# Splitting the last accumulated first-weight part directly on ScalarE and VectorE

## The chip, the cores and the metric

The kernel runs on one core of a Trainium2 chip. The metric is the device time of one launch in microseconds (us), the median over runs; the runs of the kernel before lie between 389.09 and 389.71 us. Smaller is better. A profiled execution gives the trace that is read below.

## The reference, cut to what matters

```python
x = A_x                                   # (1, 2048, 512)
xn = _layernorm(x, axis=-1)
s = irfft2(rfft2(xn) * (w_r + 1j*w_i))    # over tokens and channels
h = _layernorm(xn, axis=-1)
u = gelu(einsum("bsd,sf->bdf", h, w1) + b1)   # (1, 512, 1792)
y = einsum("bdf,fs->bds", u, w2) + b2
return x + s * silu(y.transpose(0, 2, 1))
```

Two branches share the normalised input: a spectral filter `s` (transform, multiply, transform back) and a two-layer perceptron over the token axis, whose first product is `h` by `w1` and whose second is by `w2`. All of it is in float32; the large products are made of three products of a high and a low part each.

## The kernel before, in words

The 2048 tokens are 16 tiles `j` of 128 partitions. Of the 14 column blocks of `w1` (128 columns each), seven are accumulated in the first stage, while the tiles of `x` are loaded, normalised and transformed. The other seven follow in the second stage, in two batches: `w1` is cut into 32 parts `i`, part `i` being tile `i % 16` of batch `i // 16`. A part of the second batch has 384 columns in two runs: block 6 (128 columns) and blocks 12 and 13 (256 columns). It is used by three tiles of products on TensorE (`hidden`), each of three matmuls: high by high, high by low of `h`, and low by high, in this order. The last four parts are kept and used at the end of the stage, one block after the other (lines L146 to L148).

A part needs a high half `wh` (`w1h` in the trace) and a low half `wl` (`w1l`), made from the raw weights `w` (`w1s`, three buffers) that SyncE's queue loads. There are two ways to make them, in `w1_part`:

```python
            if i in ADDED:
                A.activation(wh, w, AF.Copy)
                A.activation(wl, wh.bitcast(F32), AF.Copy, scale=-1.0)
                w1_runs(i, wl, G, accum_op=ALU.add)
                return wh, wl
            split(wh, wl, w)
```

With `split`, ScalarE rounds the high half (L143) and VectorE subtracts it from the raw weights (L143). With `ADDED`, ScalarE also writes the negated high half into `wl` (L484), and two DMAs from GpSimd's queue add the raw weights to it from memory once more (L344 on POOL). Parts 10, 12, ... 22 take the second way in the kernel before.

The parts are asked for by `hidden_rest`, three ahead of use. The order of the second stage is written out by hand: the tables `PACE` and `LAST` say how many tiles of products go between the steps of the spectral filter. The filter works on eight pairs of frequency groups, `filter_pair(n)`, with items 2n and 2n+1. Of an item, ScalarE copies `px` out of PSUM (L567); SyncE's queue exchanges partitions of it with four DMAs `xc<-px` (L573); GpSimd's queue loads the factors `wt` (L564); VectorE works through L587 to L598, with the multiplication by `wt` at L591 and the last step at L598; TensorE multiplies back with `hf,xc` (64 matmuls for a pair, the first 32 of its first item). Between these steps VectorE and ScalarE make the forms of the activated hidden layer (`forms`: `fa`, `fb`, `fc`, `fd` at L301 and L302, `u` at L321 to L324).

At the end of the second stage SyncE's queue, behind the last `w1s` loads, loads four tiles of `w2` (L696); GpSimd's queue adds a second piece of `w2` to two of them (L698). From these ScalarE and VectorE make `w2f` (L707, L708) for the third stage, which is the product with `w2`, the gate and the output.

Each engine runs its instructions in program order, and so does each DMA queue when it issues.

Of the kernel before, what the change touches and what calls it, by code (L numbers as in the profile page):

```python
# [26 lines left out]
PACE = [(2, 2, 2, 1, 1, 1)] * 4 + [(2, 2, 2, 2, 1, 1)] * 4  # L27
LAST = (4, 4, 4, 4, 4)
MADE = (3, 3, 3, 3, 3, 3, 2, 2)
ADDED = range(10, 24, 2)  # L30
WARM = 16
TAIL = 4
LATE = 12
# [101 lines left out]
def spectral_mixer_kernel(tc, x, w1, b1, w2, b2, wk, we, wx, c_f, c_ft, c_d, c_i, c_g, c_h, out):  # L135
# [14 lines left out]
    with tc.tile_pool(name="ps", bufs=1, space=PSUM) as psp, ExitStack() as left, ExitStack() as right:  # L150
# [322 lines left out]
        def w1_part(i):  # L473
# [7 lines left out]
            wh, wl = (w1p.tile([P, 4 * P], F32R, name=f"w1{c}{runs[0][0]}_{j}", tag="w1" + c)[:, :n] for c in "hl")  # L481
            if i in ADDED:
                A.activation(wh, w, AF.Copy)
# [407 lines left out]
```

## Time and profile before

| | |
|---|---|
| time, median of 3 runs | 389.25 us (389.09 to 389.71) |
| span of the profiled execution, first to last instruction | 387.8 us |
| median less span | 1.4 us |
| PE busy | 375.9 us (97%) |
| DVE busy | 323.3 us (83%) |
| ACT busy | 228.2 us (59%) |
| POOL busy | 78.4 us (20%) |
| DMA | 70.03 MB, mean 181 GB/s |

The profiled execution is known by its span alone; what lies around it is taken as the 1.4 us by which the median of the runs exceeds the span. The first stage lasts to about 97 us of the span, the second to about 215 us, the third to the end. PE, PEld, DVE, ACT, POOL and SP in the views are TensorE's matmuls, its weight loads, VectorE, ScalarE, GpSimd and SyncE; a `q` behind the name is the queue from which an engine issues DMAs. In rows of the timeline the first number is the start in the span, the second the duration, and a bracket at the end is the idle time ahead of the instruction with what ended it.

### The profile page before, as it was taken

How to read it: one execution, taken by the hardware profiler on the slowest of the kernel's cores; microseconds unless marked ns; L12 is line 12 of the kernel's file. 1: busy time of each engine (PE TensorE's matmuls, PEld its weight loads, DVE VectorE, ACT ScalarE, POOL GpSimd, SP SyncE). 2: the span in 40 equal slices, each digit the busy share in tenths (PEclk: the TensorE clock that was granted, in tenths of full speed). 3: DMA queues.
4: the chain of work that ended last, by engine and by line, in shares of the span. 5: the costliest groups of instructions: out<-in, count | busy, mean ns of one | idle time of the engine just before them, and what ended most of it. 6: DMA issues, size and time to landing. Idle time of an engine off the chain costs nothing.

```text
span 387.8 us, 8067 instructions
## 1 busy us (share of the span) xinstructions
PE 375.9 (97%) x2936; PEld 330.1 (85%) x2936; DVE 323.3 (83%) x734; ACT 228.2 (59%) x412; POOL 78.4 (20%) x133
## 2 busy tenths in 40 slices
PE   7999999999999999999699989999999999999995
PEld 4888888888777887777488979999999999999994
DVE  6899999976679998996985999797878798787873
ACT  4676776674843465575326795565656564746541
POOL 3133323221203233332001003020202020110100
PEclk9999999999999999999789999999999999999999
DMA  8965777312626889988928388997968779795602
GB/s 262 309 238 168 258 241 248 91 55 86 206 64 179 209 237 266 231 214 211 234 67 246 54 241 214 209 225 161 227 147 217 134 206 177 208 160 162 103 2 55
DMA packets 39144, 70.03 MB, mean 181 GB/s; under 512 B 5424, under 2 KB 21440, under 8 KB 38976
## 3 DMA queue, kind: packets, MB, share of 16 engines
q1 hardware_dynamic: 30048, 48.14, 39.9%
q0 software_dynamic: 9056, 21.38, 28.9%
q8 instruction: 23, 0.38, 0.4%
q14 instruction: 17, 0.14, 0.1%
HBM read 61.10 MB, written 8.13 MB: 179 GB/s over the span
## 4 chain that ended last, share of the span: by engine, by line
PE 82%; DVE 7%; DMA 4%; issue 4%; ACT 1%; POOL 1%; DVEq 0%; POOLq 0%; ACTq 0%
PE ps L829 27%; PE ps L132 24%; PE ps L377 20%; PE ps L241 4%; PE ps L764 3%; DVE w2f L708 2%; DMA out_dram<-g 2%; DMA w1l<-in_w_dram 2%; PE ps L147 2%; PE ps L366 1%; PE ps L148 1%; PE ps L146 1%; ACT w2f L707 1%; POOL w1l L344 1%; DVE cl L143 0%
## 5 line engine op out<-in xcount | busy, mean ns | idle before, releaser
L377 PE MATMUL ps<-h,w1h 128*128 128x512 f32 x224 | 58.7, 398 | 0.0
L132 PE MATMUL ps<-h,w1h 128*128 128x512 f32 x152 | 50.1, 412 | 0.0
L708 DVE TENSOR_TENSOR w2f<-s,w2f 128x896 fp32r<-128x896 f32 x32 | 34.8, 1091 | 16.3 <-ACT w2f L707 15.7
L377 PEld LDWEIGHTS ps<-h,w1h 128*128 128x128 f32 x224 | 40.9, 188 | 7.9
L829 PE MATMUL ps<-fa,w2f 128*128 128x256 f32 x336 | 43.4, 282 | 0.0
L829 PE MATMUL ps<-fb,w2f 128*128 128x256 f32 x336 | 42.5, 281 | 0.1
L829 PE MATMUL ps<-fc,w2f 128*128 128x256 f32 x336 | 41.5, 281 | 0.9 <-DVE w2f L708 0.6
L829 PEld LDWEIGHTS ps<-fa,w2f 128*128 128x128 f32 x336 | 41.6, 188 | 0.8
L829 PEld LDWEIGHTS ps<-fc,w2f 128*128 128x128 f32 x336 | 40.3, 188 | 1.4 <-DVE w2f L708 0.8
L829 PEld LDWEIGHTS ps<-fb,w2f 128*128 128x128 f32 x336 | 40.4, 188 | 0.5 <-DVE c L799 0.5
L698 POOL DMA_DIRECT2D s<-in_w_dram x16 | 13.9, 869 | 125.1 <-DVE es L769 42.6
L707 ACT ACTIVATE w2f<-s 128x896 fp32r<-128x896 f32 x32 | 30.1, 949 | 13.9 <-DVE s L721 11.0
L132 PEld LDWEIGHTS ps<-h,w1h 128*128 128x128 f32 x152 | 28.0, 194 | 10.2 <-issue 5.0
L708 DVE TENSOR_TENSOR w2f<-a,w2f 128x896 fp32r<-128x896 f32 x24 | 26.1, 1086 | 10.1 <-ACT w2f L707 10.1
L132 PE MATMUL ps<-h,w1l 128*128 128x512 f32 x76 | 30.7, 403 | 3.3 <-DMA w1l<-in_w_dram 3.3
L377 PE MATMUL ps<-h,w1l 128*128 128x512 f32 x112 | 30.6, 390 | 0.0
L707 ACT ACTIVATE w2f<-a 128x896 fp32r<-128x896 f32 x24 | 22.8, 951 | 12.1 <-PE ps L829 7.4
L377 PEld LDWEIGHTS ps<-h,w1l 128*128 128x128 f32 x112 | 21.0, 188 | 4.5
L590 DVE SCALAR_TENSOR_TENSOR xc<-xc,turn,px 128x512 f32<-128x512 f32 x32 | 23.9, 747 | 0.0
L372 DVE TENSOR_TENSOR w1l<-w1r,w1h 128x512 fp32r<-128x512 f32 (+1 forms) x32 | 20.7, 648 | 2.4 <-ACT w1h L369 2.2
L805 POOL DMA_DIRECT2D out_dram<-g x15 | 13.4, 896 | 42.3 <-DVE g L803 42.3
L795 ACT ACTIVATE g<-c,b2t 128x256 f32<-128x256 f32 x24 | 12.1, 505 | 15.6 <-DVE c L799 13.1
(128 smaller groups left out, 765.8 us busy)
## 6 DMA issues: line engine op xcount, KB each, us to landing
a<-in_w_dram SPq DMA_DIRECT2D x24, 448.0 KB, 3.9
wt<-in_wk_dram POOLq DMA_DIRECT2D x16, 512.0 KB, 5.1
s<-in_w_dram SPq DMA_DIRECT2D x16, 448.0 KB, 4.3
s<-in_w_dram POOLq DMA_DIRECT2D x16, 448.0 KB, 6.3
w1s<-in_w_dram SPq DMA_DIRECT2D x36, 128.0 KB, 3.3
w1r<-in_w_dram SPq DMA_DIRECT2D x16, 256.0 KB, 3.7
xc<-px SPq DMA_DIRECT2D x64, 64.0 KB, 4.1
x<-in_x_dram SPq DMA_DIRECT2D x15, 256.0 KB, 4.0
```

The source lines that it names most:

```text
L132: return lambda *args, **kw: self.keep(operation(*args, **kw))
L241: T.matmul(z[:, b], h[:, b * P:(b + 1) * P], c, start=True, stop=True)
L372: keep(V.tensor_sub(dst, src, hi.bitcast(F32)))
L377: T.matmul(ps[:, bank + i], w[wi][:, i * P:(i + 1) * P], hj, start=first and j == 0, stop=last and j == NJ - 1)
L590: V.scalar_tensor_tensor(to, zt, turn[:, k:k + 1], px[:, ::-1], op0=ALU.mult, op1=ALU.add)
L698: G.dma_start(t, w2_half(*added), accum_op=ALU.add)
L707: A.activation(wf[:, 0], v, AF.Copy)
L708: V.tensor_sub(wf[:, 1], v, wf[:, 0].bitcast(F32))
L764: T.matmul(pe[:, b % 2, b // 2], yt[:, b], ci[:, b], start=True, stop=True)
L795: A.activation(g[:, cols], src, AF.Silu, bias=b2t[:, j:j + 1], scale=scale)
L805: G.dma_start(out[:, j, cols], g[:, cols], accum_op=ALU.add)
L829: T.matmul(o, wf[:, wi, i], ui, start=m + a == 0 and n in (1, 2, 5), stop=m == NH - 1 and a == 2, skip_group_check=n in (6, 3, 7, 4))
```

## The change

One number of a table changes, so that part 22 (tile 6 of the second batch) is no longer in `ADDED`:

```diff
-ADDED = range(10, 24, 2)
+ADDED = range(10, 22, 2)
```

For part 22 one ScalarE activation (L484) and two accumulating DMAs of GpSimd's queue (L344; 64 and 128 KB) go, and one VectorE subtraction of 128x384 (L143) comes. The scheduler places it, and moves one other instruction. In the names below the last number is that of a buffer, and the number before it the tile or the item: `w1l6_6` is the low half of part 22, `w1s6_9` the raw weights of part 25.

On VectorE the new subtraction stands among the steps of items 12 and 13 of the spectral filter (a piece of the difference):

```order
 L590 SCALAR_TENSOR_TENSOR xc12_2267<-xc12_2267,turn_67,px12_2265 128x512
 L591 TENSOR_TENSOR xc12_2267<-xc12_2267,wt12_2211 128x1024
+L143 TENSOR_TENSOR w1l6_6_2380<-w1s6_6_2376,w1h6_6_2379 128x384
 L592 TENSOR_TENSOR xc12_2267<-xc12_2267 128x512
 L587 TENSOR_TENSOR s1_13_2329<-xc13_2276,e1_76 128x2
```

It was put behind the multiplication of item 12, ahead of everything that is left of items 12 and 13.

Further on in VectorE's order, where item 13 ends and the forms of `u3` begin, before:

```order
L598 TENSOR_TENSOR xc13_2276<-s1_13_2329 128x2
L323 SCALAR_TENSOR_TENSOR u3_1535<-u3_1535 128x256
L324 SCALAR_TENSOR_TENSOR u3_1535<-u3_1535 128x256
L302 TENSOR_TENSOR fc3_2756<-u3_1535,fc3_2756 128x2x256
L143 TENSOR_TENSOR w1l6_8_2490<-w1s6_8_2486,w1h6_8_2489 128x384
L302 TENSOR_TENSOR fb3_2755<-u3_1535,fb3_2755 128x2x256
L587 TENSOR_TENSOR s1_14_2473<-xc14_2432,e1_76 128x2
```

And the same place in the changed kernel:

```order
L598 TENSOR_TENSOR xc13_2276<-s1_13_2329 128x2
L323 SCALAR_TENSOR_TENSOR u3_1535<-u3_1535 128x256
L324 SCALAR_TENSOR_TENSOR u3_1535<-u3_1535 128x256
L143 TENSOR_TENSOR w1l6_8_2488<-w1s6_8_2484,w1h6_8_2487 128x384
L302 TENSOR_TENSOR fc3_2754<-u3_1535,fc3_2754 128x2x256
L302 TENSOR_TENSOR fb3_2753<-u3_1535,fb3_2753 128x2x256
L587 TENSOR_TENSOR s1_14_2471<-xc14_2430,e1_76 128x2
```

The subtraction of part 24 (`w1l6_8`) moved ahead of `fc3`; ScalarE's high half of part 24 moved ahead of its own `fc3` in the same way.

On SyncE's queue nothing is moved, but a wait changes. Its order before, from the loads of part 24 on, with the semaphores that each row waits for in brackets:

```order
L344 DMA w1s6_8_2486<-in_w1_dram 128x128 [waits DMAHW0_49,DVE_49]
L344 DMA w1s6_8_2486<-in_w1_dram 128x256 [waits DMAHW1_49]
L344 DMA w1s6_9_2514<-in_w1_dram 128x128 [waits DMAHW2_49,Activation_49]
L344 DMA w1s6_9_2514<-in_w1_dram 128x256 [waits DMAHW3_49]
L585 DMA hf14_2471<-in_c_h_dram 128x128 [waits DMAHW4_49,PE_49]
L751 DMA cd_64<-in_c_i_dram 128x512 [waits DMAHW5_49]
L585 DMA hf15_2496<-in_c_h_dram 128x128 [waits DMAHW6_49,PE_49]
L573 DMA xc14_2432<-px14_2430 32x512 [waits DMAHW7_49,Activation_49]
```

And in the changed kernel:

```order
L344 DMA w1s6_8_2484<-in_w1_dram 128x128 [waits DMAHW0_49,DVE_49]
L344 DMA w1s6_8_2484<-in_w1_dram 128x256 [waits DMAHW1_49]
L344 DMA w1s6_9_2512<-in_w1_dram 128x128 [waits DMAHW2_49,DVE_49]
L344 DMA w1s6_9_2512<-in_w1_dram 128x256 [waits DMAHW3_49]
L585 DMA hf14_2469<-in_c_h_dram 128x128 [waits DMAHW4_49,PE_49]
L751 DMA cd_64<-in_c_i_dram 128x512 [waits DMAHW5_49]
L585 DMA hf15_2494<-in_c_h_dram 128x128 [waits DMAHW6_49,PE_49]
L573 DMA xc14_2430<-px14_2428 32x512 [waits DMAHW7_49,Activation_49]
```

The load of part 25 takes the raw buffer of part 22. It waited for ScalarE, which read that buffer last; now it waits for VectorE's subtraction. Behind it on the queue stand the loads `hf14`, `cd` and `hf15` and the exchanges `xc14` and `xc15`.

## The prediction

> **What bounds the kernel now.** I read the engine table of the page first, then the waits and TensorE's timeline in the second half of the second stage, then the timeline of the queue that TensorE waited for, and the windows for the granted clock.
>
> ```profile
> PE 375.9 (97%) x2936; PEld 330.1 (85%) x2936; DVE 323.3 (83%) x734; ACT 228.2 (59%) x412; POOL 78.4 (20%) x133
> ```
>
> TensorE is nearly always busy, so one looks for its few waits. The longest behind the start is at the part that the change touches.
>
> ```profile
> 184.48 0.61 PE L132 MATMUL ps<-h,w1h 128*128 128x512 f32 x2
> ...
> 185.16 0.61 PE L132 MATMUL ps<-h,w1h 128*128 128x512 f32 x2
> 188.44 0.47 PE L132 MATMUL ps<-h,w1l 128*128 128x512 f32 x1 [2.67 <-DMA w1l<-in_w_dram]
> ...
> 190.00 0.80 PE L132 MATMUL ps<-h,w1l 128*128 128x512 f32 x1 [0.62 <-DMA w1l<-in_w_dram]
> 190.72 1.99 PE L132 MATMUL ps<-hf,xc 64*64 64x64 f32 x64
> 192.64 1.22 PE L132 MATMUL ps<-h,w1h 128*128 128x512 f32 x2
> ...
> 201.69 0.39 PE L132 MATMUL ps<-h,w1l 128*128 128x512 f32 x1
> ...
> 209.22 0.39 PE L148 MATMUL ps<-h,w1l 128*128 128x512 f32 x1
> ```
>
> A tile of three matmuls takes 0.68 us (184.48 to 185.16). The third of the tile begun at 185.16 reads the low half of part 22 and waits 2.67 us, that of the next tile 0.62 us, both for the accumulating DMAs. GpSimd's timeline and the chain say why they are late:
>
> ```profile
> 181.70 0.55 POOL L564 DMA_DIRECT2D wt<-in_wk_dram  x1 [7.21 <-DVE xc L591]
> 182.28 1.75 POOL L344 DMA_DIRECT2D w1l<-in_w_dram  x2
> ```
>
> ```profile
> 182.82 7.13 DMA w1l<-in_w_dram
> ```
>
> They stand in GpSimd's queue behind a load of `wt` that waited for VectorE's L591 until 181.70, and the second lands 7.13 us after 182.82. The stall has a second price, the granted clock, which is the number ahead of the last two in the rows of the windows:
>
> ```profile
> 185.00:190.00 5.00, 1.71 (x8) 0.80 (x6) 4.67 (x12) 1.02 (x3) 0.55 (x1) 0.94 1.09 292
> 190.00:195.00 5.00, 5.00 (x71) 3.96 (x72) 5.00 (x12) 3.39 (x8) 0.00 (x0) 0.50 0.64 164
> 195.00:200.00 5.00, 5.00 (x21) 4.08 (x20) 5.00 (x10) 1.05 (x2) 0.00 (x0) 0.87 0.01 2
> ```
>
> If it is either 0.50 or 1.00, means of 0.94, 0.50 and 0.87 make a stretch at half clock of 0.6 + 5.0 + 1.3 = 6.9 us, which costs 3.4 us of matmul time. So 2.67 + 0.62 + 3.4 = 6.7 us are lost at this one place. The same rows show the other side: VectorE is busy for 4.67, 5.00 and 5.00 us of 5. What it makes here is what the end of the stage waits for.
>
> **The change part by part.** ScalarE loses one activation in a stretch where it idles, worth nothing. GpSimd's queue loses two issues; nothing that is waited for stands close behind them. VectorE gains one subtraction of the form that it has elsewhere, and all else follows from VectorE:
>
> ```profile
> 174.28 0.55 DVE L143 TENSOR_TENSOR w1l<-w1s,w1h 128x384 fp32r<-128x384 f32 x1
> 174.75 0.68 DVE L302 TENSOR_TENSOR fb<-u,fb 128x512 fp32r<-128x512 f32 x1
> ...
> 180.17 1.23 DVE L591 TENSOR_TENSOR xc<-xc,wt 128x1024 f32<-128x1024 f32 x1
> ...
> 188.40 0.15 DVE L598 TENSOR_TENSOR xc<-s 128x2 f32<-128x2 f32 x1
> ...
> 188.92 0.42 DVE L324 SCALAR_TENSOR_TENSOR u<-u 128x256 f32<-128x256 f32 x1
> 189.64 0.69 DVE L302 TENSOR_TENSOR fc<-u,fc 128x512 fp32r<-128x512 f32 x1 [0.30 <-ACT fc L301]
> ...
> 191.32 0.16 DVE L587 TENSOR_TENSOR s<-xc,e 128x2 f32<-128x2 f32 x1
> ...
> 198.60 0.55 DVE L143 TENSOR_TENSOR w1l<-w1s,w1h 128x384 fp32r<-128x384 f32 x1
> ...
> 207.22 0.55 DVE L143 TENSOR_TENSOR w1l<-w1s,w1h 128x384 fp32r<-128x384 f32 x1
> ```
>
> *The low half.* The subtraction starts behind L591, at 180.17 + 1.23 = 181.40, and ends at 181.95. TensorE wants it at 185.16 + 0.45 = 185.6, so both waits go, with 3.6 us to spare.
>
> *What is late next on TensorE.* It reaches `hf,xc` at 185.16 + 2 x 0.68 = 186.5 instead of 190.72. The second item there needs L598 of item 13, ready at 188.40 + 0.15, and the subtraction pushes VectorE by its step of 0.47 (174.28 to 174.75): 189.02. So TensorE waits again, some 2 us, now for VectorE. Half of the 64 matmuls took 0.96 us at half clock (190.72 to 192.64); at that clock the next tile starts at 189.98 instead of 192.64. If the clock is again half until 196.3, a lead of 2.66 there is 1.33 afterwards. Later limits: the low half of part 26 is written at 198.60 + 0.55 and read at 201.69, that of part 31 at 207.22 + 0.55 and 209.22. With VectorE 0.17 later (next step) the lead can be at most 2.37 and 1.28. I take 1.28 at the end of the product.
>
> *VectorE itself.* The 0.47 is paid back in part: the subtraction of part 24 now fills the 0.30 for which VectorE waited ahead of `fc` at 189.64. VectorE is ready for item 14 at 191.32 + 0.47 - 0.30 = 191.49, 0.17 later.
>
> *SyncE's queue.* The load of part 25 waits for the subtraction, and item 14's exchange is behind it. The issues, and how long the exchanges took from issue to landing (item 14's four as a group; its fourth alone, issued at 184.59; and one of item 12, issued at 174.32):
>
> ```profile
> 179.64 0.85 SPq L344 DMA_DIRECT2D w1s<-in_w_dram  x2
> ```
>
> ```profile
> 180.59 1.13 SPq L585 DMA_DIRECT2D hf<-in_c_h_dram  x1
> ...
> 184.59 0.63 SPq L573 DMA_DIRECT2D xc<-px  x1
> ```
>
> ```profile
> xc<-px SPq DMA_DIRECT2D x4, 64.0 KB, 5.8
> xc<-px SPq DMA_DIRECT2D x1, 64.0 KB, 5.7
> xc<-px SPq DMA_DIRECT2D x1, 64.0 KB, 4.1
> ```
>
> Part 25 is issued at about 182.0 instead of 179.64, 2.36 later. Shifted whole, the fourth exchange is issued at 186.95; 0.8 earlier, 186.15, if the 1.13 us of `hf`, odd for one issue, happens inside the wait. It lands 4.1 to 5.8 us later, at 190.25 to 192.75, against VectorE's 191.49. So this costs between 0 and 1.26 us. I take the middle, 191.5, and with it nothing: the accumulations that shared this time are gone. The Trainium skill ("DMA: Bandwidth & Descriptors", section "Issuing engines are not separate DMA queues") speaks against this choice: DMAs of all issuing engines run on the same 16 DMA engines and interleave, so 192 KB taken from one queue and put later into the other would relieve nothing, and by it the exchange keeps its 5.8 us. The rows show both 4.1 and 5.8 and do not decide it.
>
> *The end of the stage.* VectorE's later steps follow one another, and SyncE's last loads follow VectorE's (the load of part 29 is issued at 199.19, after the subtraction at 198.60 that ends at 199.15). Behind them come the loads of `w2`. What VectorE waits for there:
>
> ```profile
> 199.19 0.33 SPq L344 DMA_DIRECT2D w1s<-in_w_dram  x1
> ```
>
> ```profile
> 209.16 0.87 POOL L698 DMA_DIRECT2D s<-in_w_dram  x1 [22.31 <-DMA s<-in_w_dram]
> ```
>
> ```profile
> s<-in_w_dram POOLq DMA_DIRECT2D x1, 448.0 KB, 5.1
> ```
>
> ```profile
> 213.93 1.09 DVE L708 TENSOR_TENSOR w2f<-a,w2f 128x896 fp32r<-128x896 f32 x1 [1.29 <-ACT w2f L707]
> ...
> 215.88 1.09 DVE L708 TENSOR_TENSOR w2f<-s,w2f 128x896 fp32r<-128x896 f32 x1
> ```
>
> ```profile
> 214.62 0.94 ACT L707 ACTIVATE w2f<-s 128x896 fp32r<-128x896 f32 x1
> ```
>
> ```profile
> 225.83 2.50 PE L829 MATMUL ps<-fc,w2f 128*128 128x256 f32 x19 [0.62 <-DVE w2f L708]
> ...
> 230.12 0.50 PE L146 MATMUL ps<-ch,cft 128*128 128x512 f32 x1 [0.63 <-ACT ch L143]
> ```
>
> The 1.29 us ahead of 213.93 is time in which VectorE waited, through ScalarE, for TensorE's last sums; a lead of TensorE shortens it. But the next `w2f` is made of the accumulated piece `s`, which lands at 209.16 + 5.1 = 214.26 whatever TensorE does. ScalarE needs 0.94 on it, two handovers an estimated 0.05 each (182.82 + 7.13 = 189.95 to the matmul at 190.00): VectorE cannot start before 215.30. It started at 215.88. The room is 0.58 us, not 6.7. From there VectorE runs without a wait into the places where TensorE stalls for it, 225.83 and 230.12, and so sets the end.
>
> *The sum*, on the span of 387.8 and so on the median, 1.4 above it: -0.58, and +0.17 for everything that VectorE and SyncE's loads are later: -0.41 us. 389.25 - 0.41 = 388.8. Bounds: from 388.7 with no delay to 389.25 + 0.17 + 1.26 - 0.58 = 390.1.
>
> **The rivals.** 0.2%, 0.78 us, is about what a measurement of this kernel can tell from no change.
>
> *All of it comes back.* 389.25 - 6.7 = 382.6. For it speaks only the size of the stall; against it the 189.02 of item 13 and 215.30. 0.04.
>
> *TensorE's lead comes through.* If the piece `s` lands earlier (5.1 us for 448 KB in a time of crowded loads), the whole lead of 1.28 us reaches the third stage: 388.0. For it: VectorE's waits at 211 to 214 do end on TensorE. Against: the loads are issued no earlier than before. 0.20.
>
> *The exchange of item 14 is the new wait* (slower). It decides from a fourth landing at 191.49 + 0.41 = 191.9 on, and at 192.75 costs 390.1. Everything behind it on VectorE, down to `w2`, is late with it. For it: 2.36 us later on a queue that issues in order. Against: the 4.1. 0.16, of which 0.09 beyond 0.2%.
>
> *The half clock moves to where it hurts* (slower). If the new wait of 2 us keeps the clock at 1.00, TensorE runs into the low half of part 26 2.4 us early and waits there. Half a clock for 6.9 us from then on loses 3.4, so that it ends the product 1.0 later than before, and VectorE's 213.93 waits on that: 390.25. Waits of 2.67 and 0.62 brought the half clock before. 0.09. The Trainium skill ("TensorE: Matmul & The Clock Gate", "Why this matters for your kernels") wants no idle gap above about 3 us; by that rule a 2 us wait halves nothing, here or at part 26. The trace disagrees in part, since 2.67 us did, with 0.62 behind it.
>
> *The change doesn't do what it says*: the subtraction is held up in VectorE's order beyond 185.6. Nothing in the rows from 178 to 182 holds it. 389.25, 0.03.
>
> **How the numbers follow.** My forecast has 0.48. Faster by over 0.2%: 0.04 + 0.20 = 0.24. Slower: 0.09 + 0.09 = 0.18. The rest, 0.58, is within: forecast, the mild part of the late exchange, no effect. The range of the forecast alone is 388.7 to 389.3. For 8 in 10 it reaches from 387.9, just under the lead that comes through, to 390.2, just over the late exchange; outside are the full return, part of the moved half clock and the tails of the two between.
>
> **What would show it.** No wait of TensorE for `w1l` by DMA at part 22; a wait of about 2 us ahead of the second half of `hf,xc`, ended by VectorE's L598 near 189.0; `xc14` landed by 191.5 and L587 started by then; `w2f<-s` on ScalarE starting right at the landing of `s`, near 214.4, with no room left. I am wrong if L587 of item 14 shows an idle time over half a microsecond, if the clock is 0.50 after 200 us, or if the first `w2f<-s` starts clear of 214 on either side.

## The result, and the profile after

| | median | lowest to highest | runs |
|---|---|---|---|
| before, beside it | 389.40 us | 388.99 to 391.63 | 12 |
| after | 389.47 us | 388.25 to 390.79 | 12 |

The ratio after to before is 0.9992, 95% interval 0.9973 to 1.0010: no change that can be told. In a second measurement, the changed kernel as `after_again` beside 35 runs of before, it is 0.9982 (0.9965 to 0.9999). The forecast, 0.41 us off 389.25, is a ratio of 0.9989.

The stall for the accumulating DMAs is gone. The profiled execution of the changed kernel has a span of 386.9 us. Its TensorE timeline at part 22 and, below it, at part 26:

```profile
187.45 0.69 PE L132 MATMUL ps<-hf,xc 64*64 64x64 f32 x32
189.64 0.79 PE L132 MATMUL ps<-hf,xc 64*64 64x64 f32 x32 [1.49 <-DVE xc L598]
...
199.86 0.50 PE L132 MATMUL ps<-h,w1l 128*128 128x512 f32 x1 [1.95 <-DVE w1l L143]
```

TensorE reaches `hf,xc` at 187.45, not 190.72, and waits there 1.49 us for VectorE, then 1.95 us at the low half of part 26, again for VectorE. Its waits of 2.67 + 0.62 us became 1.49 + 1.95. The granted clock (the number ahead of the last two) now stays whole, and VectorE fills all but 0.03 us of these 15 us:

```profile
185.00:190.00 5.00, 3.51 (x63) 2.67 (x64) 4.97 (x14) 0.05 (x1) 0.55 (x1) 1.00 0.90 264
190.00:195.00 5.00, 5.00 (x49) 4.16 (x41) 5.00 (x11) 4.13 (x9) 0.00 (x0) 1.00 0.74 218
195.00:200.00 5.00, 3.05 (x14) 2.21 (x13) 5.00 (x11) 0.65 (x2) 0.00 (x0) 1.00 0.07 23
```

VectorE's timeline at the new subtraction, at item 13's last step, at item 14's first, and at `w2f`:

```profile
182.00 0.55 DVE L143 TENSOR_TENSOR w1l<-w1s,w1h 128x384 fp32r<-128x384 f32 x1
...
189.43 0.15 DVE L598 TENSOR_TENSOR xc<-s 128x2 f32<-128x2 f32 x1
...
190.30 0.55 DVE L143 TENSOR_TENSOR w1l<-w1s,w1h 128x384 fp32r<-128x384 f32 x1
190.76 0.69 DVE L302 TENSOR_TENSOR fc<-u,fc 128x512 fp32r<-128x512 f32 x1
191.37 0.69 DVE L302 TENSOR_TENSOR fb<-u,fb 128x512 fp32r<-128x512 f32 x1
191.97 0.15 DVE L587 TENSOR_TENSOR s<-xc,e 128x2 f32<-128x2 f32 x1
...
215.34 1.09 DVE L708 TENSOR_TENSOR w2f<-s,w2f 128x896 fp32r<-128x896 f32 x1 [0.78 <-ACT w2f L707]
```

In ScalarE's timeline the first `w2f<-s` now waits for the accumulated piece:

```profile
214.35 0.95 ACT L707 ACTIVATE w2f<-s 128x896 fp32r<-128x896 f32 x1 [1.03 <-DMA s<-in_w_dram]
```

The chain that ended last shows the handover best. Before, it ran over part 22's DMA and 16.63 us of TensorE:

```profile
182.82 7.13 DMA w1l<-in_w_dram
190.00 16.63 PE ps L132 x175
```

After, it runs through VectorE, SyncE's queue and the two transfers of `s`, and TensorE is out of it. (The view infers what released an instruction. What SyncE's last loads of `w1s` wait for is a raw buffer that a subtraction gives back: that of part 28 ran from 201.47 to 202.02, and the first load of part 31 was issued at 202.05.)

```profile
202.72 0.43 DVE u L321
203.16 0.41 SPq L344
...
204.72 3.97 DMA s<-in_w_dram
...
209.25 5.08 DMA s<-in_w_dram
...
214.35 0.96 ACT w2f L707
...
215.34 1.09 DVE w2f L708
```

Absolute times need care. In this execution the second stage began later than in the one of before, as the `hf,xc` group of items 10 and 11 shows (TensorE's timeline, before, then after), 177.40 against 178.25. The 0.85 us are there from the start: the sixteen matmuls at the head of the span take 5.15 us before and 6.03 after.

```profile
2.00 5.15 PE L366 MATMUL ps<-wz 128*128 128x512 bf16 x16 [2.00 <-POOL wz L354]
...
177.40 1.22 PE L132 MATMUL ps<-hf,xc 64*64 64x64 f32 x64
```

```profile
2.01 6.03 PE L366 MATMUL ps<-wz 128*128 128x512 bf16 x16 [2.01 <-POOL wz L354]
...
178.25 1.22 PE L132 MATMUL ps<-hf,xc 64*64 64x64 f32 x64
```

So the table below counts from this group, which lies ahead of everything that the change moves. "Half clock" is the sum of the shares lost in the windows behind, as in the prediction. The first matmul with `cft` is the one at 230.12 before and 229.58 after.

| kernel | TensorE waits near 183 to 191 | half clock behind | wait at part 26 | VectorE starts first `w2f<-s` | first `cft` | ratio to before |
|---|---|---|---|---|---|---|
| before | 2.67 + 0.62, DMA | 6.9 | 0 | 38.48 | 52.72 | 1 |
| after | 1.49, VectorE | 0 | 1.95 | 37.09 | 51.33 | 0.9992 |
| `after_again` | 1.65, VectorE | 3.4 | 0.32 | 38.15 | 52.38 | 0.9982 |
| `s1_first_before` | 2.53, DMA | 0 | 0.33 | 36.49 | 50.74 | 0.9993 |
| `s1_first_after` | 1.11, VectorE | 0 | 1.94 | 36.81 | 51.04 | 0.9991 |
| `wt14_later` | 1.83, VectorE | 3.4 | 0.83 | 37.93 | 52.17 | 1.0000 |
| `cap_off_before` | 1.90, DMA | 0 | 0.99 | 36.39 | 50.61 | 0.9977 |
| `cap_off_after` | 1.72, VectorE | 3.4 | 0.35 | 37.12 | 51.35 | 0.9964 |
| `part22_free` | 1.74, VectorE | 3.4 | 0.80 | 37.83 | 52.07 | 0.9986 |
| `light_after` | 1.32, DMA | 0 | 0 | 36.18 | 50.42 | 0.9938 |
| `light_cap_off_after` | 2.20, DMA | 0 | 0 | 34.43 | 48.67 | 0.9936 |

The last two columns of times differ by 14.22 to 14.25 us in every row: whatever happened before, the third stage is set by VectorE's first `w2f<-s`.

The group leaves one thing in. VectorE's own run through the stage begins with L587 of item 12, which waits for that item's exchange (before, then after):

```profile
178.53 0.16 DVE L587 TENSOR_TENSOR s<-xc,e 128x2 f32<-128x2 f32 x1 [3.09 <-DMA xc<-px]
```

```profile
179.21 0.16 DVE L587 TENSOR_TENSOR s<-xc,e 128x2 f32<-128x2 f32 x1 [2.76 <-DMA xc<-px]
```

In the kernels in which VectorE does all its work this is 0.46 to 1.65 us behind the group, from execution to execution. Counted from this L587, VectorE starts the first `w2f<-s` at 37.35 us before, 36.13 after, 37.02 in `after_again`, 35.86 and 36.23 in the two `s1_first` kernels, 36.28 in `wt14_later`, 36.24 in `part22_free` and 35.93 in both `cap_off` kernels.

The 0.89 us between after and `after_again` is the road of `s`, not the clock. TensorE is not on the chain of `after_again` there; SyncE issued the load of `s` 0.17 us later behind that L587, and the load took 4.66 us where it took 3.97:

```profile
204.90 4.66 DMA s<-in_w_dram
...
210.13 5.10 DMA s<-in_w_dram
```

### The profile page after: what moved, and what is told of

The parts are those of the page before. It is cut to its first block, busy times and chain, and to the rows that moved or that the text cites. A ratio compares the mean times of both kernels' runs of the same rounds, so it can differ in the third digit from the quotient of the medians.

```text
span 386.9 us, 8060 instructions
## 1 busy us (share of the span) xinstructions
PE 374.0 (97%) x2936; PEld 327.8 (85%) x2936; DVE 323.9 (84%) x735; ACT 227.7 (59%) x411; POOL 76.8 (20%) x131
## 4 chain that ended last, share of the span: by engine, by line
PE 77%; DMA 9%; DVE 7%; issue 3%; SPq 2%; ACT 1%; POOL 1%; DVEq 0%; POOLq 0%; ACTq 0%
PE ps L829 27%; PE ps L377 20%; PE ps L132 19%; DMA s<-in_w_dram 4%; PE ps L241 4%; PE ps L764 3%; DMA xc<-px 2%; DMA out_dram<-g 2%; PE ps L366 2%; DVE w2f L708 2%; PE ps L147 1%; SPq L573 1%; DVE xc L590 1%; PE ps L148 1%; ACT w2f L707 1%
## 5 line engine op out<-in xcount | busy, mean ns | idle before, releaser
L377 PE MATMUL ps<-h,w1h 128*128 128x512 f32 x224 | 58.7, 398 | 0.0
L132 PE MATMUL ps<-h,w1h 128*128 128x512 f32 x152 | 48.7, 402 | 0.0
L377 PEld LDWEIGHTS ps<-h,w1h 128*128 128x128 f32 x224 | 40.9, 188 | 7.9
L132 PEld LDWEIGHTS ps<-h,w1h 128*128 128x128 f32 x152 | 27.2, 188 | 9.8 <-issue 5.0
L132 PE MATMUL ps<-h,w1l 128*128 128x512 f32 x76 | 29.8, 392 | 2.0 <-DVE w1l L143 2.0
L377 PE MATMUL ps<-h,w1l 128*128 128x512 f32 x112 | 30.6, 389 | 0.0
L564 POOL DMA_DIRECT2D wt<-in_wk_dram x16 | 8.8, 553 | 63.0 <-DVE xc L591 51.1
```

Source lines behind the costliest of these rows:

```text
L132: return lambda *args, **kw: self.keep(operation(*args, **kw))
L377: T.matmul(ps[:, bank + i], w[wi][:, i * P:(i + 1) * P], hj, start=first and j == 0, stop=last and j == NJ - 1)
L564: G.dma_start(wt, wk[:, i])
```

## The experiments

Theory A: beside the stall runs a second path that is almost as long, so that only the small difference can be gained. VectorE is busy without a break behind part 22, and through SyncE's queue it also sets when the piece `s` lands; freed of the DMA, TensorE only waits for VectorE instead. The rivals: the landing of `s` binds by itself, VectorE's added subtraction eats the gain, or the half clock does.

**The change again, and an earlier `s`.** In the two `s1_first` kernels SyncE issues the load of `s` ahead of that of `a`:

```diff
-        nxt = {"a12": w2_load("a12", w2p, 0, 1), "s1": s1_load(0, w2p), ...
+        nxt = {"s1": s1_load(0, w2p), "a12": w2_load("a12", w2p, 0, 1), ...
```

> The changed kernel once more, beside the others on one chip. My theory (the gain is capped by the accumulated piece s of w2, whose landing VectorE waits for): 0.2 to 0.6 us below the kernel before, ratio 0.9985 to 0.9995; the first w2f<-s on ScalarE starts within 0.1 us of the landing of s, after an idle time of about 1 us. Rival (TensorE's lead comes through): 1.3 us below, ratio 0.9967.

> The kernel before, with the load of the piece s of w2 issued ahead of the load a12, so that its accumulation starts and lands about 1 us earlier. Cap theory: in the kernel before VectorE comes to w2f<-s without a wait (215.88, behind fa), held back by TensorE's late sums, so an earlier s buys nothing: 0.0 +- 0.2 us against the kernel before. Rival (the w2 loads bound the third stage in both kernels): about 1 us faster here too.

> The changed kernel with the same earlier load of s. Cap theory: the wait of 0.78 us of VectorE ahead of w2f<-s goes, so this one is 0.8 to 0.9 us below the changed kernel and 1.2 to 1.4 us below the kernel before (ratio about 0.9967). Rival (VectorE's own chain, not the landing of s, sets the end): same as the changed kernel, ratio 0.999.

Ratios 0.9982 (0.9965 to 0.9999), where 0.9985 to 0.9995 was expected, 0.9993 (0.9968 to 1.0017) and 0.9991 (0.9969 to 1.0013). Neither the 0.8 to 0.9 us that `s1_first_after` was to gain over the changed kernel nor the rival's 1 us shows. The swap is a weak lever: counted from the `hf,xc` group, GpSimd's issue for `s` came 0.6 to 0.9 us earlier than after, but the addition took 5.4 us instead of 5.1, so that `s` landed 35.5 and 35.8 us behind the group against 36.1. But the profiled execution of `s1_first_before` shows what was not planned: the same stall for the same DMA, and no half clock behind it. Its TensorE timeline and windows:

```profile
189.46 0.47 PE L132 MATMUL ps<-h,w1l 128*128 128x512 f32 x1 [2.53 <-DMA w1l<-in_w_dram]
...
199.89 0.50 PE L132 MATMUL ps<-h,w1l 128*128 128x512 f32 x1 [0.33 <-DVE w1l L143]
```

```profile
190.00:195.00 5.00, 4.95 (x80) 3.71 (x79) 4.70 (x11) 3.92 (x9) 0.00 (x0) 1.00 0.72 196
195.00:200.00 5.00, 4.67 (x22) 3.54 (x21) 5.00 (x11) 1.10 (x3) 0.00 (x0) 1.00 0.07 24
```

After 2.53 us lost to the DMA, TensorE still had 0.33 us to wait at part 26 for VectorE, and ScalarE waited 0.48 us for `s`. So in this execution, at full clock, the stall that the change removes costs nothing, since TensorE catches VectorE up. In the execution of before, with 6.9 us of half clock behind the stall, TensorE did not catch up, and its chain runs over the stall: the first `w2f<-s` came at 37.35 behind VectorE's L587 there, 1.2 to 1.5 us later than in `s1_first_before` and after.

**The cause of the stall.** Item 14's `wt` load goes behind part 22's two DMAs in GpSimd's queue:

```diff
-                w1_runs(i, wl, G, accum_op=ALU.add)
+                w1_runs(i, wl, Kept(G, keep) if i == 22 else G, accum_op=ALU.add)
...
-            G.dma_start(wt, wk[:, i])
+            if i != 14:
+                G.dma_start(wt, wk[:, i])
             yield
+            if i == 14:
+                keep(G.dma_start(wt, wk[:, i]))
```

`keep` holds an instruction at its place in the order of the program.

> The kernel before, part 22 still accumulated, but its two DMAs stand ahead of the load wt14 in GpSimd's queue. If the stall at part 22 came from the place in that queue (behind wt14, which waits for L591 until 181.7) and not from the accumulation as such, TensorE has no wait for w1l, with no subtraction added on VectorE: it then waits 1 to 1.5 us for L598 at hf,xc, and the end is as in the changed kernel or up to 0.3 us earlier, capped by s: 0.4 to 0.6 us below the kernel before. Rival (accumulation is too slow at any place): the wait for w1l stays over 1 us and the time is that of the kernel before.

Ratio 1.0000 (0.9979 to 1.0021). No matmul waits for `w1l` accumulated by DMA any more, so the place in the queue was the cause of the stall; TensorE waits 1.83 us ahead of the second `hf,xc` half instead, and 0.83 us at part 26. The row of the first wait puts it down to a DMA, but VectorE's last step of item 13 (L601 in this kernel) starts 0.22 us ahead of it, as L598 does after (189.43 and 189.64):

```profile
190.27 0.79 PE L132 MATMUL ps<-hf,xc 64*64 64x64 f32 x32 [1.83 <-DMA cd<-in_c_i_dram]
```

```profile
190.05 0.16 DVE L601 TENSOR_TENSOR xc<-s 128x2 f32<-128x2 f32 x1
```

So this wait too was for VectorE. The stall went here without a change on VectorE, and no gain shows; the 0.4 to 0.6 us that were expected are within the interval.

**Part 22 for free.** The low half of part 22 stays the negated high half: the stall's DMAs go, and no subtraction comes.

```diff
-                w1_runs(i, wl, G, accum_op=ALU.add)
+                i == 22 or w1_runs(i, wl, G, accum_op=ALU.add)
```

> The kernel before with part 22's two accumulating DMAs left out (its low part stays minus the high part): no wait of TensorE for w1l, and no added work on VectorE either; it is what the change would be if VectorE's subtraction cost nothing. Theory A: TensorE then waits for VectorE's correction of xc (1.0 to 1.6 us) as in the changed kernel, s lands at 214.3 as ever, and the time is that of the changed kernel within 0.3 us. Theory C (the 0.55 us of VectorE are what the change costs): the first cft matmul comes 0.5 us earlier after the hf group of item 10 than in the changed kernel, and the time is 0.5 us below it.

389.39 us, a ratio of 0.9986 (0.9969 to 1.0002) beside 0.9992 and 0.9982 for the changed kernel; the times alone could not tell the 0.5 us of theory C. TensorE waits 1.74 us for L598 and 0.80 us at part 26. The traces decide it: from L587 of item 12 VectorE needs 12.79 us to that of item 14 here, 12.76 after and 12.79 before, and 36.24 us to `w2f<-s`, 36.13 after. VectorE's 0.55 us is not what ate the gain; theory C falls.

**Without the accumulation into `s`.** The second summand of the first `s` is left out:

```diff
-        nxt = {..., "s1": s1_load(0, w2p), ...
+        nxt = {..., "s1": w2_load("s1", w2p, NP, 0), ...
```

> The changed kernel without the accumulation into the first w2 piece s (its second summand is left out), so s is complete at its plain landing, near 208.7 instead of 214.3. Theory A (the landing of s sets the start of the third stage): ScalarE's w2f<-s no longer waits 1.03 us for the DMA, VectorE's w2f<-s starts right behind fa, 0.8 us earlier, and the first cft matmul comes 0.8 us earlier after the hf group of item 10 than in the changed kernel (51.3 us with no half clock, now about 50.5), with 14.24 us between VectorE's w2f<-s and that matmul as in every run so far; the time falls by 0.5 to 0.9 us. Theory B (TensorE or VectorE bind there, s is a bystander): the first cft matmul stays at 51.0 to 51.4 us after that group and the time within 0.2 us.

> The kernel before with the same summand of s left out. Theory A: where a half-clock window follows part 22's wait, s was not waited for (ScalarE and VectorE had no idle time ahead of it), so the first cft matmul stays 52.7 us after the hf group of item 10 and the time is the same within 0.3 us; where no half clock comes, VectorE's w2f<-s moves up by at most 0.25 us. The difference between the two kernels thus grows from 0.4 us to about 1 us. Theory B: the difference between the two kernels stays at 0.4 us or less.

388.77 us, 0.9964 (0.9946 to 0.9981), and 389.09 us, 0.9977 (0.9957 to 0.9998). In the changed kernel the waits are gone (ScalarE's and VectorE's timelines of `cap_off_after`):

```profile
214.30 0.94 ACT L707 ACTIVATE w2f<-s 128x896 fp32r<-128x896 f32 x1
```

```profile
214.95 0.69 DVE L302 TENSOR_TENSOR fa<-u,fa 128x512 fp32r<-128x512 f32 x1
215.56 1.08 DVE L708 TENSOR_TENSOR w2f<-s,w2f 128x896 fp32r<-128x896 f32 x1
```

`cft` comes 1.03 us earlier than in `after_again` (51.35 against 52.38), but no earlier than after (51.33): 50.5 was expected, and 51.35 is what theory B gave. Counted from VectorE's L587 of item 12, `w2f<-s` comes 0.2 us earlier than after and 1.1 us earlier than in `after_again`, where `s` was late. By the ratios the changed kernel fell by 0.7 to 1.1 us where theory A had 0.5 to 0.9 and theory B at most 0.2, but the intervals overlap. So that `s` is waited for is shown, and that it holds the end by the 0.8 us expected in every execution is not. That before fell by about 0.9 us and not by less than 0.3 was not expected: its profiled execution had no half clock either and might, with `s` accumulated, have waited as `s1_first_before` did. An interval of 0.4% does not let the two be told apart, and that the gap between the kernels grows is not shown.

**Less work for VectorE.** VectorE's multiplication by `wt` is left out for items 12 to 15:

```diff
-            V.tensor_mul(xv, xv, wt)
+            i < 12 and V.tensor_mul(xv, xv, wt)
```

> The changed kernel without the summand of s and without VectorE's multiplication by the filter weights in items 12 to 15 (four instructions of 1.22 us are left out, some of VectorE's neighbouring steps change places). Theory A (VectorE's load behind part 22 and the landing of s hold the rest of TensorE's lead): TensorE's waits for VectorE at 189.6 and 199.9 (1.49 and 1.95 us) shrink below 0.5 us each, the first w2 matmul comes 2 to 3 us earlier, and the time falls by 1.5 to 3 us below the changed kernel. Theory D (the lead is lost to something else, for example the loads of the w2 pieces, or the clock): the time falls by less than 1 us.

> The changed kernel without VectorE's multiplication by the filter weights in items 12 to 15 (4 instructions of 1.22 us), with the accumulation into s kept. Theory A (VectorE holds the SyncE queue, since its splits give back the first-weight buffers, and so holds the landing of s too): the first w2 piece is issued near 201.1 instead of 204.2, s lands about 10.2 us later, near 211.3, before VectorE is through with fa, and the time is that of the kernel without VectorE's multiplications and without the accumulation, within 0.3 us: about 2 us below the changed kernel. Theory E (the landing of s stands at 214.3 on its own): VectorE's w2f<-s stays near 215.3 and the time is at most 0.4 us below the changed kernel.

387.18 us, 0.9936 (0.9910 to 0.9962), and 387.85 us, 0.9938 (0.9913 to 0.9964): by the ratios 1.7 to 2.2 us below the changed kernel, with or without the accumulation. In `light_after` SyncE issues the load of `s` 22.5 us behind VectorE's L587 of item 12 (202.52 - 180.03) and not 25.5 (204.72 - 179.21), and the piece lands earlier too, at 32.6 and not at 35.1:

```profile
202.52 0.37 SPq L696 DMA_DIRECT2D s<-in_w_dram  x1
```

```profile
207.36 0.86 POOL L698 DMA_DIRECT2D s<-in_w_dram  x1 [27.23 <-DMA s<-in_w_dram]
```

```profile
212.69 0.95 ACT L707 ACTIVATE w2f<-s 128x896 fp32r<-128x896 f32 x1 [2.16 <-DMA s<-in_w_dram]
```

So the landing of `s` does not stand at 214.3 by itself (theory E falls): it follows VectorE by some 10 us of transfers. Theory A was off in one point, that `s` would then be early enough; ScalarE still waited 2.16 us for it. The scheduler moved some of VectorE's steps as well, which these two runs don't separate from the work left out. TensorE's long wait is now at 183.09 or 184.32, once more for accumulated low halves, of an earlier part, part 20; what it costs was not tried.

**Versions meant to win.** `pool_sub22` and `pool_sub_many` give subtractions to GpSimd, `pool_sum_after` the sums of the first two pieces `s`:

```diff
+            if i in SUBBED:      # i == 22, or SUBBED = (22, 23, 25, 27, 29)
+                A.activation(wh, w, AF.Copy)
+                G.tensor_sub(wl, w, wh.bitcast(F32))
+                return wh, wl
```

```diff
-        nxt = {..., "s1": s1_load(0, w2p), ..., "s4": w2_load("s4", w2p, 0, 1, (NP, 1))}
+        nxt = {..., "s1": w2_load("s1", w2p, NP, 0), ..., "s4": w2_load("s4", w2p, NP, 1)}
+        G.tensor_add(nxt["s1"], nxt["s1"], nxt["s4"]), G.tensor_add(nxt["s4"], nxt["s4"], nxt["a12"])
```

> The changed kernel with part 22's subtraction on GpSimd instead of VectorE (same values). Theory A: no DMA is waited for and VectorE is spared 0.55 us ahead of item 13's later steps: TensorE's wait for VectorE's correction of xc shrinks from 1.1 to 1.7 us by up to 0.55 us, and the time is 0 to 0.6 us below the changed kernel. Theory F (GpSimd's subtraction is slow, or holds VectorE up, or holds the wt load of item 14 that is queued behind it): TensorE waits at part 22 again or VectorE's instructions beside it grow, and the time is the changed kernel's or above.

> The changed kernel with the subtractions of parts 22, 23, 25, 27 and 29 on GpSimd (same values): 2.75 us less on VectorE between 180 and 205 us. Theory A: TensorE's waits for VectorE near 189.6 and 199.9 go down, the w2 loads are issued 1 to 2.5 us earlier, VectorE's w2f<-s too, and the time is 0.8 to 2.3 us below the changed kernel. Theory F (GpSimd is slow at it or VectorE beside it): at most 0.3 us below, or slower.

> The changed kernel, values the same, with the sums of the first two w2 pieces (s of L711 and L712) made by GpSimd additions of loaded pieces instead of accumulating DMAs; the scheduler also moves some steps of the third stage. Theory A (s is what holds the third stage): the two summands land near 208.7 and 210.9, the addition takes about 2.3 us (896 columns at the 1.00 us that GpSimd took for 384), so s is there near 213.2 instead of 214.3 to 215.2, VectorE's w2f<-s starts right behind fa, and the time is 0.4 to 0.8 us below the changed kernel. Theory G (GpSimd's addition holds up VectorE's subtraction beside it, as VectorE's steps grew beside GpSimd's subtractions, or the moved steps of the third stage cost more): the time is the changed kernel's within 0.3 us, or above it.

389.98 us, 0.9995 (0.9978 to 1.0013); 390.60 us, 1.0019 (0.9997 to 1.0042); 392.96 us, 1.0064 (1.0033 to 1.0094). None wins. In `pool_sub22` the wait for L598 shrinks to 0.85 us and the next, at part 26, is 2.33 us. In `pool_sub_many` the wait for L598 grows to 3.00 us: a VectorE step of 0.15 us, the L588 of item 13, took 1.04 us beside a GpSimd subtraction of 1.01, as theory F had it. In `pool_sum_after` the additions took 2.21 and 2.20 us, as expected, but beside them two VectorE steps grew (GpSimd's timeline, then VectorE's):

```profile
211.07 2.21 POOL L712 TENSOR_TENSOR s<-s,s 128x896 f32<-128x896 f32 x1 [24.07 <-DMA s<-in_w_dram]
213.36 2.20 POOL L712 TENSOR_TENSOR s<-s,a 128x896 f32<-128x896 f32 x1
```

```profile
211.22 2.35 DVE L302 TENSOR_TENSOR fd<-u,fd 128x256 fp32r<-128x256 f32 x1
213.49 3.02 DVE L708 TENSOR_TENSOR w2f<-a,w2f 128x896 fp32r<-128x896 f32 x1
216.43 0.41 DVE L302 TENSOR_TENSOR fd<-u,fd 128x256 fp32r<-128x256 f32 x1
```

The same forms take 0.42 and 1.09 us alone: 1.93 us lost on each. Theory G's first half is shown. The first `cft` stands 17.00 us behind `w2f<-s` there, not the 14.2 of the table, since the scheduler moved steps of the third stage; that was not tried apart.

## Why the prediction was right, point by point

*The low half in time: right.* The subtraction started at 182.00, with the stage 0.85 late (181.40 was forecast), and no matmul waited for part 22.

*TensorE's new wait: right in kind.* It came at the second half of `hf,xc`, for L598, 1.49 us for the forecast 2. The half clock that the prediction carried over from before did not come in this execution and came for 3.4 us in `after_again`. Without it TensorE's lead was larger, and the low half of part 26 took it back in 1.95 us, the limit that the prediction had placed there.

*VectorE 0.17 later: worked out in the right way, both terms a little off.* From L587 of item 12 to that of item 14 VectorE took 12.76 us (191.97 - 179.21), before 12.79 (191.32 - 178.53), so it was not later at all. From L591 of item 12 to L598 of item 13 it took 8.57 us (189.43 - 180.86) and not 8.23 (188.40 - 180.17): the subtraction pushed it by 0.34, not 0.47, since before L592 started 1.26 us behind L591 and the subtraction starts 1.14 behind it. From L598 to L587 of item 14 it took 2.54 us and not 2.92, so that 0.38 came back, not 0.30; the subtraction at 190.30 filled the idle time ahead of `fc`.

*The exchange of item 14: right that it costs nothing, wrong on its duration.* Its four transfers, as a group:

```profile
xc<-px SPq DMA_DIRECT2D x4, 64.0 KB, 3.0
```

The fourth, issued at 186.79, took 2.4 us, so that it landed near 189.2, some 2.8 us ahead of VectorE's 191.97. The span of 4.1 to 5.8 us, read from a time of crowded queues, was the wrong bound. The Trainium skill ("DMA: Bandwidth & Descriptors", section "Issuing engines are not separate DMA queues") was weighed as keeping 5.8 us; this run shows 3.0. It does not speak against the page: the loads that shared the 16 engines were others by then.

*The limit by `s`: right as the thing that ends the gain, wrong as a fixed time.* "Lands at 214.26 whatever TensorE does" held for TensorE: VectorE's `w2f<-s` was forecast at 215.30 and came at 215.34. But that agreement is luck in part, since a stage 0.85 us late met a load of 4.0 us instead of 5.0. The landing follows VectorE's splits through SyncE's queue, as `light_after` showed. The room of 0.58 us was a difference of two numbers from a single execution, while the start of VectorE's `w2f<-s` varies between 36.5 and 38.2 us behind the `hf,xc` group among the other kernels with the accumulation and VectorE's full work, and was 38.5 in the execution that the prediction was read from.

*The sum.* -0.41 us, a ratio of 0.9989, lies inside both measured intervals. One of them holds 1 and the other ends at 0.9999, so that the changed kernel is faster at all is not shown, and a size of 0.4 us cannot be confirmed by these times.

*The rivals.* All coming back (382.6) and the late exchange are dead. The moved half clock came halfway: the new wait did leave the clock at 1.00 and TensorE did run into part 26, but no half clock followed there. It did follow the wait at part 26 in `pool_sub22` and `pool_sum_after`, so the step is possible; what it costs was not told apart there. The lead that comes through needs an earlier `s`; `cap_off_after` puts this at 0.7 to 1.1 us by the ratios and 0.2 to 1.1 by the traces, around the 0.8 by which that rival lay below the forecast.

*What stays open.* The runs of one kernel spread over 4 us, more than any of these effects. Parts of it lie outside the stage: the group begins at 177.40 to 178.58 in the profiled executions, and from the first `cft` to the end of the span the kernels of the table take 157.2 to 159.5 us. The half clock is not the explanation: of 110 runs of before, the 21 with a mean granted clock of 0.999 or 1.000 have a median of 390.89 us, the other 89 one of 390.00. Whether the change makes half-clock windows rarer isn't shown either (mean clock 0.995 in 24 runs after, 0.996 in 110 before).

## What to carry to other kernels

A stall of the busiest engine is worth only the time until that engine meets the next one that is late: before counting it, look for the engine that is never idle behind it, here VectorE. Follow the work of that engine through the queues as well, since a buffer that it gives back late delays a load, and what the load brings is waited for some 10 us on. And compare stages from a common mark ahead of the change, best from the first step of the engine that sets the pace, because one execution reaches the stage about a microsecond later than the next.

## What was not expected of the hardware

The half clock does not follow from the length of a wait alone; it matters where the wait falls. In the clock's records in the traces each half-clock stretch behind the start and ahead of the end of the span lasts 3.41 us, or twice that in before. It begins 184.32 us behind the change to full clock at the head of the span in six executions, 194.56 us behind it in two, and once more 221.86 in one of these: 54, 57 and 65 times 3.413 us. That change comes 5.0 to 7.6 us into the span, from execution to execution (5.12 before, 6.90 after). So the clock seems to be decided at points 3.41 us apart, which lie elsewhere against the work each time. The windows between such points, first of `after_again`, then of `s1_first_before`:

```profile
187.54:190.95 3.41, 1.76 (x67) 1.47 (x60) 3.38 (x11) 0.99 (x2) 0.34 (x1) 1.00 0.79 219
190.95:194.36 3.41, 3.41 (x10) 2.67 (x9) 3.41 (x9) 2.65 (x7) 0.00 (x0) 0.50 0.73 175
194.36:197.77 3.41, 3.41 (x16) 2.81 (x15) 3.41 (x7) 1.30 (x3) 0.00 (x0) 1.00 0.20 59
```

```profile
185.12:188.54 3.42, 1.82 (x9) 1.16 (x7) 3.42 (x8) 0.00 (x0) 0.55 (x1) 1.00 1.03 281
188.54:191.95 3.41, 2.44 (x68) 1.70 (x68) 3.08 (x8) 2.29 (x5) 0.00 (x0) 1.00 1.04 284
```

The 1.65 us of `after_again` lie in one window, and the next is at half clock. The 2.53 us of `s1_first_before` are cut into 1.61 and 0.92, and none follows. Waits of 1.72, 1.74, 1.83, 1.94, 2.33 and 3.00 us in one window each brought the half clock too, as did the 2.67 us of before, of which 2.41 lie in one. Those of 1.90 (`cap_off_before`), 2.20 (`light_cap_off_after`) and 1.94 (`s1_first_after`, part 26) are cut by a point and did not, nor did the undivided 1.49 of after. One case does not fit: of the 1.95 us of after at part 26, 1.81 lie in one window, and no half clock followed. So the rule is not complete.

The Trainium skill ("TensorE: Matmul & The Clock Gate", section "HAM oscillation — how this bites in real kernels") wants no idle gap above some 3.4 us; the 3.4 us agrees with the length of these windows, but not as the gap from which they come: 1.65 us were enough.

A GpSimd operation on two operands in SBUF stopped VectorE's nearly as long as both ran: in `pool_sum_after` 0.42 became 2.35 us beside one of 2.21, which is 1.93 lost of the 2.06 in which they overlapped. The Trainium skill ("SBUF — State Buffer", section "SBUF: two separate sides") calls the port pair that the two engines share an exclusive lock, and these rows agree.
